# An attention kernel whose loads leave in bursts at TensorE's program fetches, with weights used as loaded and dummy matmuls in the first wait

## The chip, the cores and the metric

One core of one Trainium2 chip. The metric is the device time of one execution in microseconds (us). The engines: TensorE (matmuls; PE in the profile, PEld is its weight load), VectorE (DVE), ScalarE (ACT), GpSimd (POOL), SyncE (SP, which here issues all DMA loads). A kernel's executions scatter by some 3% here, a few by far more (before, in e1's rounds: 439.0 to 454.3 us in 38 runs, 569.6 in one), so each time is given as a median with its range. A run over 1.5% above the fastest of the same kernel is called slow (or in the slow state); verdicts rest on ratios of fast runs made in the same rounds.

## The reference, cut to what matters

Multi-head attention over a cache: x is 8 x 112 x 640, K and V are 8 x 32 heads x 512 x 192, all bf16.

```python
q = transpose((x @ wq).reshape(B, Sq, H, Dh), 0, 2, 1, 3)
scores = einsum("bhqd,bhkd->bhqk", q, k_cache) * (Dh ** -0.5)
p = softmax(scores)
o = einsum("bhqk,bhkd->bhqd", p, v_cache)
return transpose(o, 0, 2, 1, 3).reshape(B, Sq, H * Dh) @ wo
```

## The kernel before

The work is cut into 64 units u, each four heads of one batch entry. A group g of eight units shares a block of wq and wo. Per unit, K is 786 KB and V is 786 KB, each loaded in two halves; there are four buffers for each. On TensorE a unit is: S(u), 96 small matmuls (192 instructions with their weight loads) of query against transposed K; PV(u-1), 16 matmuls of the softmaxed scores against V; some Q or O matmuls (projections for other units); T(u-1), six transposes of the normalised output.

```python
for u in range(NU + 1):                       # TensorE
    if u < NU: do_S(u)
    if u > 0: do_PV(u - 1)
    for it in items_at[u][0]: do(it)          # Q or O
    if u > 0: do_T(u - 1)                     # waits for VectorE's do_NM(u - 1)
    for it in items_at[u][1]: do(it)

for u in range(NU + 1):                       # VectorE
    for t in kts[:2]: do_KT(u + 2, t)         # transposes of K, first wait for its load
    if u > 0: do_NM(u - 1)                    # normalise the output of u - 1
    for t in kts[2:3]: do_KT(u + 2, t)
    # ... O results, last KT
```

In VectorE's program the normalisation of u-1 stands behind the first two K transposes of u+2: if that K is late, so is the normalisation, and with it T(u-1) on TensorE (17.7 us in 17 waits in the trace of before). SyncE issues the loads on events of the work:

```python
for u in range(NU):                           # SyncE
    W(sp, pS, 4 * (u + 1))                    # S(u) is done
    if u + 3 < NU: load_k(u + 3, 0)
    W(sp, pPV, u)                             # PV(u-1) is done
    if u + 3 < NU: load_k(u + 3, 1)
    # ... pieces of wq and wo for later groups
    if items_at[u][0]: after(items_at[u][0][-1])
    if u + 2 < NU: load_v(u + 2, 0)
    if items_at[u][1]: after(items_at[u][1][-1])
    if u + 2 < NU: load_v(u + 2, 1)
```

## Time and profile before

| | before |
|---|---|
| time, median of 3 (range) | 443.99 us (443.99 to 452.72) |
| TensorE busy | 399.6 us, 90% |
| DMA | 118.71 MB, 84.3% of 16 engines' span |
| VectorE's wait for K | 38.3 us in 21 waits |
| TensorE stopped for no visible wait ("issue") | 10.6 us in 9 gaps |
| S block of the first / fourth unit starts | 18.4 / 48.0 us |

Two kinds of line matter. A wait line reads "engine, line, waits for whom: total us, times, longest". "issue" as releaser means that the engine waited for no semaphore. In the trace of before, TensorE's seven such gaps over 0.5 us all stand where a page of its program ends, and it goes on 2.3 to 3.3 us after the start of a program packet (see "How the fetch was read"); so I read them as its own program that had not come, and call them program gaps. The prediction shows these lines. Four more of before are needed later. The waits after the fourth S block alone (48 to 444 us), one group line of the page (busy us, mean ns, idle before) and the page's line of K loads (KB each, median us from issue to landing), each in this order:

```profile
DVE kt L952 <- DMA kr<-in_k_cache_dram: 21.3, 17, 2.1
PE ps L863 <- DVE os L964: 9.1, 15, 1.3
```

```profile
L952 DVE STREAM_TRANSPOSE kt<-kr 128x384 int32<-128x384 int32 x256 | 208.8, 864 | 88.7 <-PE ps L840 50.4 <-DMA kr<-in_k_cache_dram 38.3
```

```profile
kr<-in_k_cache_dram SPq DMA_DIRECT2D x128, 384.0 KB, 4.3
```

### The profile page before, as it was taken

Reading aid. Unit: us, or ns where it says so; the run is one execution under the profiler, and the core shown is the slowest. Engines: PE = TensorE matmul, PEld = TensorE weight load, DVE = VectorE, ACT = ScalarE, POOL = GpSimd, SP = SyncE. Lnnn points to the kernel's source line nnn. Section 1 sums busy time; section 2 is a strip of 40 time slices with the busy share of each in tenths; the row PEclk is TensorE's granted clock in tenths of the full one; section 3 lists DMA queues with packets and bytes.
Section 4 is the critical chain, followed back from the end, with each engine's and each line's share of the span. In section 5 each row is a group of like instructions: output and inputs, shape, how many; then the busy total and the mean of one; then the engine's idle time right before and its main releaser. Section 6 shows DMA issues by size and latency. Waiting matters only on the chain.

```text
span 444.3 us, 20578 instructions
## 1 busy us (share of the span) xinstructions
PE 399.6 (90%) x8920; PEld 293.0 (66%) x8920; DVE 317.5 (71%) x634; ACT 220.8 (50%) x421; POOL 76.8 (17%) x280
## 2 busy tenths in 40 slices
PE   4956999989979999998999899879999999998992
PEld 3534677767767677766676677657677777766771
DVE  2443678768776678886787588756788867887942
ACT  3533355555553655555454555436455565455540
POOL 1040222112211022211221022110222100111110
PEclk9998799999998999999999999989999999999998
DMA  7879799998887989998799899878889988999731
GB/s 263 250 260 332 228 281 299 298 324 278 281 266 245 295 286 299 298 354 262 217 308 297 288 295 284 277 232 257 288 281 306 286 261 272 292 284 298 217 130 36
DMA packets 100655, 120.07 MB, mean 270 GB/s; under 512 B 5584, under 2 KB 84176, under 8 KB 100560
## 3 DMA queue, kind: packets, MB, share of 16 engines
q1 hardware_dynamic: 100560, 118.71, 84.3%
q8 instruction: 71, 1.16, 1.1%
q14 instruction: 24, 0.20, 0.1%
HBM read 117.54 MB, written 1.15 MB: 267 GB/s over the span
## 4 chain that ended last, share of the span: by engine, by line
PE 68%; DMA 16%; DVE 6%; issue 5%; SPq 2%; POOL 1%; ACT 0%; DVEq 0%; POOLq 0%
PE ps L854 17%; PE ps L821 16%; PE ps L840 15%; DMA kr<-in_k_cache_dram 14%; PE ps L805 13%; PE ps L863 5%; DVE os L964 3%; DVE kt L952 3%; PE ps L810 1%; DMA wqr<-in_wq_dram 1%; POOL wqs L1041 1%; DMA xs<-in_x_dram 1%; SPq L1070 1%; SPq L1076 1%; PE ps L785 1%
## 5 line engine op out<-in xcount | busy, mean ns | idle before, releaser
L952 DVE STREAM_TRANSPOSE kt<-kr 128x384 int32<-128x384 int32 x256 | 208.8, 864 | 88.7 <-PE ps L840 50.4
L910 ACT ACTIVATE pT<-ps 128x448 bf16<-128x448 f32 x256 | 118.6, 548 | 79.4 <-PE ps L840 79.4
L821 PE MATMUL ps<-wos,oT 128*128 128x320 bf16 x672 | 109.6, 300 | 1.1 <-ACT oT L919 0.8
L854 PE MATMUL ps<-vs,pT 128*128 128x193 bf16 x1024 | 99.4, 249 | 6.1 <-issue 5.0
L840 PEld LDWEIGHTS ps<-qT,kt 32*128 32x128 bf16 x6144 | 78.5, 94 | 24.3 <-issue 20.2
L805 PE MATMUL ps<-xT,wqs 128*128 128x448 bf16 x420 | 93.5, 359 | 0.9 <-issue 0.8
L840 PE MATMUL ps<-qT,kt 32*128 32x112 bf16 x6144 | 89.1, 210 | 5.3 <-issue 4.6
L854 PEld LDWEIGHTS ps<-vs,pT 128*128 128x128 bf16 x1024 | 83.9, 98 | 12.9 <-issue 7.1
L902 ACT ACTIVATE qT<-ps 128x448 bf16<-128x448 f32 x96 | 52.2, 545 | 66.2 <-PE ps L805 56.9
L821 PEld LDWEIGHTS ps<-wos,oT 128*128 128x128 bf16 x672 | 63.1, 98 | 29.0 <-issue 1.4
L919 ACT ACTIVATE oT<-ps 128x672 bf16<-128x672 bf16 x64 | 46.8, 731 | 63.3 <-PE ps L863 63.2
L1052 POOL TENSOR_SCALAR bad<-rinv 112x4 f32<-112x4 f32 x64 | 14.6, 228 | 322.8 <-DVE rinv L960 322.8
L964 DVE TENSOR_TENSOR os<-ps,rinv 112x768 bf16<-112x768 f32 x64 | 61.3, 958 | 2.5 <-DVE rinv L960 0.4
L805 PEld LDWEIGHTS ps<-xT,wqs 128*128 128x128 bf16 x420 | 39.9, 99 | 29.0 <-issue 3.3
L863 PE MATMUL ps<-ident,os 112*128 112x112 bf16 x384 | 30.4, 216 | 17.9 <-DVE os L964 17.7
L863 PEld LDWEIGHTS ps<-ident,os 112*128 112x128 bf16 x384 | 21.0, 99 | 34.9 <-DVE os L964 34.0
L978 DVE TENSOR_TENSOR acc<-ps,acc 128x320 f32<-128x320 f32 x84 | 40.3, 480 | 1.5 <-PE ps L821 1.5
L1041 POOL COPY wqs<-wqr 128x384 bf16<-128x384 bf16 x70 | 33.2, 507 | 24.3 <-DMA wqr<-in_wq_dram 22.4
L957 DVE TENSOR_REDUCE sm<-ps 112x4 f32<-112x8 f32 x64 | 10.1, 158 | 11.7 <-PE ps L854 11.5
L810 PE MATMUL ps<-xT,wqs 128*32 128x448 bf16 x240 | 15.8, 422 | 1.2 <-ACT xT L891 0.8
L1053 POOL TENSOR_SCALAR bad<-rinv 112x4 f32<-112x4 f32 x64 | 14.5, 226 | 4.0
L960 DVE RECIPROCAL rinv<-sm 112x4 f32<-112x4 f32 x64 | 11.4, 178 | 3.4
(30 smaller groups left out, 52.0 us busy)
## 6 DMA issues: line engine op xcount, KB each, us to landing
kr<-in_k_cache_dram SPq DMA_DIRECT2D x128, 384.0 KB, 4.3
vs<-in_v_cache_dram SPq DMA_DIRECT2D x128, 384.0 KB, 4.6
wos<-in_wo_dram SPq DMA_DIRECT2D x48, 160.0 KB, 4.3
wqr<-in_wq_dram SPq DMA_DIRECT2D x35, 192.0 KB, 4.4
out_dram<-xs SPq DMA_DIRECT2D x7, 160.0 KB, 1.9
wqs<-in_wq_dram SPq DMA_DIRECT2D x1, 960.0 KB, 6.5
xs<-in_x_dram SPq DMA_DIRECT2D x1, 640.0 KB, 4.3
xs<-in_x_dram SPq DMA_DIRECT2D x1, 480.0 KB, 7.9
```

The costliest lines, as they stand in the source:

```text
L805: mm = pe.matmul(ps[:, bank(it), 0:HQ], wqs[:, g % 2, dc, 128 * c:128 * (c + 1)], rhs, start=(dc == 0), stop=(dc == DC - 1))
L821: mm = pe.matmul(ps[:, bank(it), 0:HO], oT[:, c, 128 * m:128 * (m + 1)], wos[:, g % 2, c, HO * h:HO * (h + 1)], start=(c == 0), stop=(c == 5))
L840: mm = pe.matmul(ps[:, a, SQ * t:SQ * (t + 1)], kt[u % 2][p, t, c // 2, :, c % 2], qT[g % 2][p, c, SQ * b:SQ * (b + 1)], start=(c == 0), s ...
L854: mm = pe.matmul(pv[:, k, e, o0:o0 + DH + 1], pT[u % 2][:, a, t, :], vs[u % NV][:, a, t // 2, v0:v0 + DH + 1], start=(t == 0), stop=(t == ...
L863: mm = pe.transpose(psb[:, 4, o0:o0 + SQ], os_[u % 2][:, 128 * j:128 * (j + 1)], ident[0:SQ, 0:SQ])
L902: act.activation(qT[g % 2][:, c, HQ * h:HQ * (h + 1)], ps[:, bank(it), 0:HQ], ACTF.Copy).then_inc(aQ, 1)
L910: act.activation(pT[u % 2][:, a, :, 0:SQ], ps[:, a, 0:4 * SQ].rearrange("p (t q) -> p t q", t=4), ACTF.Exp, scale=scale).then_inc(aEX, 1)
L919: act.activation(oT[:, :, SQ * b:SQ * (b + 1)].rearrange("p (k c) q -> p k c q", k=2), src.rearrange("p k (c q) -> p k c q", c=3), ACTF.Co ...
L952: dve.transpose(dst, src).then_inc(vKT, 1)
L964: dve.tensor_tensor(os_[u % 2][:].rearrange("p (k e d) -> p k e d", k=2, e=2), pv[0:SQ, :, :, 1:1 + DH], rinv[:, u % 4, :].rearrange("p (k ...
L978: ins = dve.tensor_tensor(ob[:, m, cs] if g == NG - 1 else acc[:, m, cs], src, acc[:, m, cs], op=ALU.add)
L1041: ins = gp.tensor_copy(wqs[:, g % 2, dc, :].rearrange("p (k e a i) -> p e k a i", k=3, e=2, a=4)[:, e], wqr[:, dc, :].rearrange("p (a k i ...
```

## The change

The intent: let a count of TensorE's own instructions tell when it has entered a new page of its program (256 instructions by the places of the gaps, see "How the fetch was read"; a program packet is 16.3 KB), and let SyncE issue everything that is due just then. The next page's fetch should then be ahead of the burst in the queues, and the burst over before the fetch after it. Besides: wq is read by strided matmul operands as it was loaded, where GpSimd had reordered it; K is transposed in the matching order; nine dummy matmuls fill the first wait, meant to have TensorE's clock up when work comes (the first three Q took 1.86 us each before, and 1.0 us with the dummies).

```diff
+    FIRST = 194
+            def put(emit, first, us):            # every matmul and transpose goes through this
+                at[0] += len(held) // 2
+                held.clear()
+                mm = emit()
+                if first and at[0] >= 256 * len(fetch) + FIRST:
+                    mm.then_inc(pF, 1)           # "a page was entered"
+                    fetch.append(at[1])
+                at[0] += 2
   ... cut ...
-                    for a in range(4):           # first weight block: quarter-width matmuls
-                        w0 = DH * a + 64 * (c // 2) + c % 2
-                        mm = pe.matmul(ps[32 * a:32 * a + 32, bank(it), 0:HQ], wqs[:, 0, dc, w0:w0 + 63:2], rhs, ...)
+                    mm = matmul(0.188, ps[:, bank(it), 0:HQ], wqs[:, g % 2, dc, c::6], xT[:, dc, HQ * h:HQ * (h + 1)], ...)
   ... cut ...
+            for _ in range(9):
+                matmul(0.43, ps[:, 7, :], zero[:, 0:128], zero[:], start=True, stop=True)
   ... cut ...
-                src = kr[u % NK][:, t:16:4, :].bitcast(I32).rearrange("p s (c i) -> p c s i", c=3)
+                src = kr[u % NK][:, t:16:4, :].bitcast(I32).rearrange("p s (i c) -> p c s i", c=3)
   ... cut: GpSimd's reorder() goes; x tiles in other PSUM banks ...
-            for u in range(NU):
-                W(sp, pS, 4 * (u + 1))
-                if u + 3 < NU:
-                    load_k(u + 3, 0)
   ... cut: the whole loop over events ...
+            loads = [(0.0, load_k, 2, 0), (0.0, load_k, 2, 1), (0.3, load_v, 1, 0), (0.3, load_v, 1, 1)]
+            loads += [(0.1, load_wq, 1, c) for c in range(DC)] + [(1.0, load_wo, 0, c) for c in range(6)]
+            for u in range(NU):
+                g, b = divmod(u, B)
+                if u + 3 < NU:
+                    loads += [(u, load_k, u + 3, 0), (u + 0.25, load_k, u + 3, 1)]
+                if u + 2 < NU:
+                    loads += [(u + 0.5, load_v, u + 2, 0), (u + 0.75, load_v, u + 2, 1)]
   ... cut: wq and wo likewise ...
+            loads.sort(key=lambda w: w[0])
+            for n, us in enumerate(fetch):
+                ...                              # place = unit reached by then
+                due = [w for w in loads if w[0] <= place + 0.45]
+                if due:
+                    sp.wait_ge(pF, n + 1)
+                for _, fn, p0, p1 in due:
+                    fn(p0, p1)
+                loads = loads[len(due):]
```

## The prediction

> **What bounds the kernel now.** I read the page first (engine shares, slices, queues), then the table of waits, then the timeline of TensorE around its gaps, then the DMA view and the busy table for short stretches there. The page:

> ```profile
> PE 399.6 (90%) x8920; PEld 293.0 (66%) x8920; DVE 317.5 (71%) x634; ACT 220.8 (50%) x421; POOL 76.8 (17%) x280
> GB/s 263 250 260 332 228 281 299 298 324 278 281 266 245 295 286 299 298 354 262 217 308 297 288 295 284 277 232 257 288 281 306 286 261 272 292 284 298 217 130 36
> q1 hardware_dynamic: 100560, 118.71, 84.3%
> q8 instruction: 71, 1.16, 1.1%
> ```

> TensorE is the bound, with DMA close behind: 118.71 MB in 444 us, and one slice that reached 354 GB/s. At that rate the bytes would need 335 us, so DMA need not bind if it is kept fed. The q8 line is the program itself: 1.16 MB / 71 is 16.3 KB a packet, and 17,840 matmuls and weight loads / 71 is 251 per packet.

> The table of waits says what stops TensorE:

> ```profile
> DVE kt L952 <- DMA kr<-in_k_cache_dram: 38.3, 21, 7.5
> PE ps L863 <- DVE os L964: 17.7, 17, 4.6
> PE ps L785 <- DMA xs<-in_x_dram: 5.2, 1, 5.2
> PE ps L854 <- issue: 5.0, 4, 2.1
> PE ps L840 <- issue: 4.6, 3, 2.8
> PE ps L805 <- issue: 0.8, 1, 0.8
> PE ps L821 <- issue: 0.2, 1, 0.2
> ```

> VectorE stands 38.3 us because K tiles land late; 17.7 us of that reaches TensorE, since the normalisation (L964) stands behind the K transposes in VectorE's order. The four "issue" rows (10.6 us) are gaps in which TensorE waits for no semaphore. The longest, in the timeline of TensorE:

> ```profile
> 290.96 1.35 PE L840 MATMUL ps<-qT,kt 32*128 32x112 bf16 x94
> 295.15 0.22 PE L840 MATMUL ps<-qT,kt 32*128 32x112 bf16 x2 [2.84 <-issue]
> 295.38 1.58 PE L854 MATMUL ps<-vs,pT 128*128 128x193 bf16 x16
> 296.76 2.07 PE L805 MATMUL ps<-xT,wqs 128*128 128x448 bf16 x5
> ```

> It stops two matmuls short of a block's end, where no wait stands in the program. The DMA view of 292.7 to 293.9 us has this line, which the view of 290.9 to 292.7 has not:

> ```profile
> q8 instruction: 1, 0.02, 4.9%
> ```

> So a program packet moved inside the gap, behind 1.8 us of data at full queues: TensorE had run out of program. After such gaps it also runs at half clock (the Q above took 2.07 us; elsewhere 1.11). The busy table of chosen stretches gives the granted clock:

> ```profile
> 33.90:37.30 3.40, 3.40 (x70) 1.86 (x71) 1.26 (x2) 1.27 (x2) 0.00 (x0) 0.51 0.94 270
> 44.10:50.90 6.80, 5.46 (x111) 3.87 (x112) 2.96 (x8) 1.74 (x4) 0.65 (x3) 0.50 0.76 246
> 296.70:300.10 3.40, 3.40 (x14) 1.70 (x12) 2.44 (x6) 0.54 (x1) 0.65 (x3) 0.50 0.79 242
> ```

> With a fourth stretch like the last (at 132.8), half of the busy time in these is lost: (3.4 + 5.5 + 3.4 + 3.2) / 2 = 7.7 us.

> [...]

> **The change, part by part.**

> *Loads tied to the program fetch.* TensorE's first accumulating matmul after each 256-instruction boundary bumps a semaphore; SyncE then issues all loads due. The fetch request is ahead of the burst, and the burst should be over before the next fetch. A page is about one unit of work (a unit is 272 to 280 instructions), so 5.3 us or a little more. Working through the list that the kernel builds, usual bursts are 3 to 6 loads, 1.2 to 1.95 MB, or 3.4 to 5.5 us at 354 GB/s, plus 1.5 us or so to land (the 160 KB stores, on quiet queues, take 1.9 us in all). The fullest spill 1 to 1.5 us into the next page, whose fetch (about 1 us) still has 4 us of room. So I expect the 10.6 us of "issue" to fall to about 2. K halves go out 0.8 to 1.4 units before VectorE may use them, near the front of the burst when they are late, so against 4.3 us from issue to landing they are mostly in time: of 9.3 us waits L863 <- L964 after the third unit I keep 4.

> *The start.* Nine 512-column matmuls at half clock (about 0.43 us each, 3.9 us) fill the 5.2 us in which TensorE waits for x. They cost nothing; the clock should be full near 6.6 to 8 us in place of 13.4. The first Q can't start before the first weights are there (issued at 1.24, 6.5 us to landing: 7.8). Today it starts at 8.34, the first three Q run at 1.86 us each, and the first S starts at 18.41. Full-width Q cost 5 x 0.189 = 0.945 against 20 quarter-width ones in 1.04. New order: three Q from 7.9 to 10.7, the late x tiles land near 11, Q, Q, transpose, Q to 14; K transposes of the first unit follow the fifth x tile and end near 13.7. First S at about 14.4: 4 us won.

> *The first three units.* Today S starts at 18.4, 23.2, 36.3 and 48.0: the third and fourth wait 4.65 and 3.98 us for late K and run half-clocked. At full rate the units cost S 1.29 + three Q 2.84 = 4.1; + PV 1.46 = 5.6; + transposes and the rest = 6.0. So S would start at 14.4, 18.6, 24.2, 30.2. The first burst is heavy, though (12 loads, 3.7 MB, 10.6 us at 354): V of the second unit is near its end and lands about 1 us after its need, and the next fetch waits behind it. I add 3 us: 33.2 against 48.0, 14.8 us won, with the start's 4 in it.

> *Weights as loaded.* The 70 copies on GpSimd (33.2 us, off the path except near 24.9 to 29.5) vanish; so does the wait of loads for them. The strided weight load hides behind a 0.187 us matmul; K transposes should keep 0.86 us. I count 0 for both.

> *After the fourth S (48.0).* 396.3 us remain today. In them: "issue" 9.8 (10.6 less 0.9 at 24.7, rounded), waits for L964 9.3 (17.7 less 4.65 and 3.98, with short ones that I counted from the timeline), half clock (2.9 + 3.2 + 3.4) / 2 = 4.8. Together 23.9, leaving 372.4 if all went. I keep 2 of issue, 4 of K waits, 0 of clock: 378.4.

> Sum: 33.2 + 378.4 = 411.6; I say **411 us** (before / after 1.08). If nothing at all were kept it would be 30.2 + 372.4 = 402.6.

> **The rivals.**

> *VectorE becomes the bound.* It is busy 317.5 / 64 = 5.0 us a unit, against 5.7 to 6.0 of TensorE. If the stride of 12 bytes made the 256 transposes a quarter slower (0.86 to 1.08), it would need 5.8 us a unit, and any late K would go straight through: 420 to 430 us. For it: VectorE's narrow room. Against: [...]the destination is already written at a stride of 4 int32.

> *DMA becomes the bound.* Loads end about 25 us before the kernel does, so at 411 us they must average 118.7 / 380 = 312 GB/s, where the page shows 245 to 332 in most slices. Gaps between bursts waste rate, and bursts that overlap catch up with the fetch again. Then K is late once more, and the time is 418 to 430. For it: 84.3% share already. Against: the 354 slice, and slices below 260 fall where loads were held back by events.

> *The alignment misses.* The count assumes 62 instructions before the kernel's own first one. If a boundary lies elsewhere, the burst goes ahead of the fetch at every page instead of some, and "issue" grows: 71 pages x 0.5 us would be 35 us, at or above 435. Against: the constant looks fitted[...].

> **Range and chances.** The floor of 402.6 and the small rivals set 403 to 424. All named gains together are 41 us and 2% is 8.9, so most of them would have to fail: faster 0.93, same 0.05, slower 0.02.

> **What would show it.** Right: "issue" before TensorE under 3 us; VectorE's wait for K from 38.3 to under 15; no half clock after the start; first S near 14.4 and fourth near 33; K transposes still 0.86 us; Q at 0.95 us. Wrong: transposes near 1.1 us or Q above 1.1 (stride); issue gaps at every page (alignment); DMA share near 100% with K waits as today (DMA bound).

## The result, and the profile after

The changed kernel took 460.81 us (median of 4, 456.92 to 465.36) against 444.93 us of the kernel before in the same rounds: **3.3% slower**. All ratios in this document are the mean time of one kernel's fast runs over that of the other's fast runs of the same rounds, so they are not quite the ratio of the medians: here 1.0335, 95% interval 1.0230 to 1.0441. The first profile fell in the slow state, so I ran the unedited kernel once more, later in the study:

> The changed kernel once more, without any edit, because its one profile fell in the slow state and its few times scatter, so that the padded run could not be set against it. Both theories: time 456 to 463. If page phase is worth time, this is 4 us or more above the padded run (457.8, scattered 453 to 463) in a profile of the fast state, that is at or above 456 against 451.6; if it is not, the two profiles agree within 2 us. K wait 50 to 60 and issue 17 to 22 in a fast profile.

It took 454.16 us (453.64 to 461.30), ratio 1.0325 (1.0205 to 1.0445): the same verdict, a little under the times that I had expected. Its profile is of the fast state, and the lines below are of it. First the page: busy time, bandwidth in 40 slices, queues, and the shares of the chain that ended last.

```profile
PE 401.5 (89%) x8749; PEld 303.2 (67%) x8749; DVE 320.0 (71%) x635; ACT 220.3 (49%) x421; POOL 43.5 (10%) x210
GB/s 280 246 345 249 309 285 298 246 255 305 305 302 288 266 243 234 298 266 316 290 306 267 221 268 337 288 303 259 325 193 264 268 303 284 283 263 277 188 62 35
q1 hardware_dynamic: 100560, 118.71, 81.4%
PE 44%; DMA 28%; DVE 12%; issue 8%; SPq 6%; ACT 1%; DVEq 0%
```

TensorE is no busier (401.5 against 399.6 us) and DMA moves the same bytes at a lower share (81.4 against 84.3%). Time went into waiting. The waits, to be set against those in the prediction:

```profile
DVE kt L974 <- DMA kr<-in_k_cache_dram: 53.8, 34, 5.3
PE ps L803 <- DVE os L986: 20.3, 25, 5.4
PE ps L800 <- issue: 14.9, 9, 3.0
PE ps L800 <- ACT pT L932: 2.4, 1, 2.4
PE ps L803 <- DMA xs<-in_x_dram: 0.2, 1, 0.2
```

VectorE's wait for K rose from 38.3 to 53.8 us instead of falling below 15; TensorE's gaps for lack of program rose from 10.6 to 14.9 us instead of falling to 2 (to 17.3 with the row for ScalarE's pT, see below). The wait for x is gone, as meant (5.2 to 0.2). After the fourth S block alone (42.6 to 452 us) the two K rows are, against 21.3 and 9.1 above:

```profile
DVE kt L974 <- DMA kr<-in_k_cache_dram: 38.9, 30, 2.6
PE ps L803 <- DVE os L986: 12.7, 23, 1.2
```

Half of all units now find their K late. The page's line of K loads says part of why: a K half takes 5.1 us to land where it took 4.3.

```profile
kr<-in_k_cache_dram SPq DMA_DIRECT2D x128, 384.0 KB, 5.1
```

The start, in the timeline of TensorE (start, duration, what, count, idle before), then one line of VectorE's:

```profile
8.10 3.01 PE L800 MATMUL ps<-xT,wqs 128*128 128x448 bf16 x15 [0.88 <-ACT xT L913]
...
15.82 1.36 PE L800 MATMUL ps<-qT,kt 32*128 32x112 bf16 x96 [0.73 <-ACT qT L924]
...
23.27 2.06 PE L800 MATMUL ps<-xT,wqs 128*128 128x448 bf16 x10
30.76 0.74 PE L803 MATMUL ps<-ident,os 112*128 112x112 bf16 x6 [5.44 <-DVE os L986]
...
42.58 2.03 PE L800 MATMUL ps<-qT,kt 32*128 32x112 bf16 x96
```

```profile
27.95 1.53 DVE L974 STREAM_TRANSPOSE kt<-kr 128x384 int32<-128x384 int32 x2 [2.69 <-DMA kr<-in_k_cache_dram]
```

The first three Q take 1.0 us each in place of 1.86, and the first S block starts at 15.8 us (18.4 before). But the fourth unit's K lands at 27.9 us; the normalisation stands behind its transposes, T waits 5.44 us, and the clock falls (0.54 granted from 30.7 to 34.1 us). The fifth unit's K, asked for after V and six pieces of wo, lands at 37.5 us and T waits again (2.08 us). The fourth S block starts at 42.6 us, and runs at half clock itself (2.03 us for what takes 1.36). Last, the program: one gap later on, and the granted clock and bandwidth of five stretches (columns: window, length, busy of PE, PEld, DVE, ACT, POOL, granted clock, DMA share, GB/s).

```profile
159.01 1.36 PE L800 MATMUL ps<-qT,kt 32*128 32x112 bf16 x96
163.42 2.71 PE L800 MATMUL ps<-vs,pT 128*128 128x193 bf16 x16 [3.04 <-issue]
```

```profile
30.70:34.10 3.40, 3.34 (x59) 1.95 (x63) 1.49 (x3) 1.28 (x2) 0.00 (x1) 0.54 1.08 369
41.00:44.40 3.40, 3.40 (x98) 2.23 (x99) 0.72 (x2) 1.09 (x2) 0.00 (x0) 0.55 0.14 42
163.80:167.20 3.40, 3.40 (x20) 2.55 (x19) 0.96 (x4) 0.00 (x0) 0.44 (x2) 0.54 0.52 160
334.50:337.90 3.40, 3.16 (x19) 2.74 (x20) 0.34 (x2) 0.00 (x0) 0.00 (x0) 0.54 0.36 96
423.20:426.60 3.40, 3.40 (x18) 1.97 (x17) 2.50 (x8) 0.00 (x0) 0.65 (x3) 0.54 0.12 15
```

The gaps are as long as before (3.04 us here, 2.84 the longest then), and the clock still falls after some (0.54 after the one shown). In the last column DMA moves 369 GB/s in the first half-clock stretch, then 42, 160 and 96 (the last comes when nearly everything is loaded). In three such stretches of the kernel before it moved 242 to 270 GB/s, but in the fourth, after a program gap, only 129:

```profile
133.10:136.50 3.40, 3.40 (x19) 2.69 (x20) 0.74 (x4) 0.00 (x0) 0.29 (x2) 0.54 0.38 129
```

By the program, loads that leave only when TensorE enters a page stop when TensorE stops. What that costs is not shown by these few stretches.

One more program gap goes under another name. At 332.34 us TensorE stops for 2.41 us, again where a page ends, and goes on 2.51 us after a packet. The profile puts it down to ScalarE's pT (the row in the waits above), but the PV that follows needs only pT of the unit before, for which S had already waited. So it is a program gap too. The same row stands in most other runs, with one exception of 0.7 us (in e10) at page ends and 2.2 to 3.0 us after a packet; the kernel before has none.

### The profile page after: what moved, and what is told of

Its sections match the earlier page's. It is cut to its first block, busy times and chain, and to the rows that moved or that the text cites. A ratio compares the mean times of both kernels' runs of the same rounds, so it can differ in the third digit from the quotient of the medians.

```text
span 463.7 us, 19950 instructions
## 1 busy us (share of the span) xinstructions
PE 402.9 (87%) x8749; PEld 303.9 (66%) x8749; DVE 320.4 (69%) x635; ACT 220.1 (47%) x421; POOL 43.1 (9%) x210
## 3 DMA queue, kind: packets, MB, share of 16 engines
q1 hardware_dynamic: 100560, 118.71, 80.0%
## 4 chain that ended last, share of the span: by engine, by line
PE 48%; DMA 26%; DVE 12%; issue 9%; SPq 3%; ACT 1%; DVEq 0%
PE ps L800 43%; DMA kr<-in_k_cache_dram 26%; DVE kt L974 7%; PE ps L803 4%; DVE os L986 4%; SPq L1085 1%; SPq L1099 1%; SPq L1091 1%; ACT pT L932 1%; DVE rinv L982 1%; SPq L1078 0%; ACT oT L941 0%; DVE ps L983 0%; ACT xT L913 0%; DVE sm L979 0%
## 5 line engine op out<-in xcount | busy, mean ns | idle before, releaser
L800 PE MATMUL ps<-wos,oT 128*128 128x320 bf16 x672 | 111.3, 304 | 3.5 <-issue 2.6
L800 PE MATMUL ps<-xT,wqs 128*128 128x448 bf16 x480 | 107.2, 361 | 1.8 <-ACT xT L913 0.8
L800 PEld LDWEIGHTS ps<-vs,pT 128*128 128x128 bf16 x1024 | 83.7, 98 | 27.2 <-issue 18.6
L800 PEld LDWEIGHTS ps<-qT,kt 32*128 32x128 bf16 x6144 | 77.7, 93 | 18.9 <-issue 14.8
L800 PE MATMUL ps<-qT,kt 32*128 32x112 bf16 x6144 | 87.8, 209 | 0.7 <-ACT qT L924 0.7
L800 PEld LDWEIGHTS ps<-xT,wqs 128*128 128x128 bf16 x480 | 56.8, 126 | 26.0 <-issue 3.3
L1062 POOL TENSOR_SCALAR bad<-rinv 112x4 f32<-112x4 f32 x64 | 14.4, 225 | 399.3 <-DVE rinv L982 399.3
L803 PEld LDWEIGHTS ps<-ident,os 112*128 112x128 bf16 x384 | 21.3, 100 | 44.0 <-DVE os L986 42.6
L1000 DVE TENSOR_TENSOR acc<-ps,acc 128x320 f32<-128x320 f32 x84 | 39.9, 475 | 2.4 <-PE ps L800 2.2
L979 DVE TENSOR_REDUCE sm<-ps 112x4 f32<-112x8 f32 x64 | 10.1, 158 | 23.4 <-PE ps L800 23.4
L1065 POOL TENSOR_TENSOR cnt<-cnt,bad 112x8 f32<-112x8 f32 x64 | 12.8, 200 | 5.3
L1000 DVE TENSOR_TENSOR xs<-ps,acc 128x320 bf16<-128x320 f32 x14 | 6.3, 482 | 2.2 <-PE ps L800 2.2
```

The lines of the kernel that those rows point to most:

```text
L800: return put(lambda: pe.matmul(out, w, m, start=start, stop=stop, **kw), start and not stop, us)
L803: return put(lambda: pe.transpose(out, m, eye), first, 0.05)
L1000: ins = dve.tensor_tensor(ob[:, m, cs] if g == NG - 1 else acc[:, m, cs], src, acc[:, m, cs], op=ALU.add)
L1062: gp.tensor_scalar(bad[:, 0, :], rinv[:, u % 4, :], LO, None, op0=ALU.is_lt)
L1065: gp.tensor_tensor(cnt[:], cnt[:], bad[:], op=ALU.add).then_inc(gC, 1)
```

## The experiments

Fourteen runs, one of them the changed kernel again, in five calls (no e5 is on record). A first table gives the results together; "gaps" is the sum of TensorE's issue rows, and after the plus the program gaps that the profile puts down to pT. Times of different calls are compared through their ratios to the kernel before.

| run | what | median (range), us | ratio, 95% interval | K wait | gaps |
|---|---|---|---|---|---|
| before | | 444.1 to 446.1 by call | 1 | 38.3 | 10.6 |
| changed | repeat | 454.2 (453.6 to 461.3) | 1.0325 (1.0205 to 1.0445) | 53.8 | 14.9 + 2.4 |
| e1 | changed, loads on old events | 443.6 (438.4 to 451.4) | 0.9993 (0.9953 to 1.0034) | 34.0 (slow) | 18.3 + 2.2 (slow) |
| e2 | changed, bursts 64 instructions later | 457.6 (455.2 to 460.9) | 1.0293 (1.0193 to 1.0393) | 44.0 | 22.3 + 3.0 |
| e3 | changed, K earlier in the bursts | 440.7 (437.8 to 504.0) | 0.9943 (0.9894 to 0.9993) | 13.3 | 17.2 + 2.7 |
| e4 | changed, slivers of K and V (wrong result) | 423.9 (423.3 to 424.5) | 0.9552 (0.9442 to 0.9662) | 12.8 | 5.4 + 2.9 |
| e6 | e1 with K a unit earlier | 434.8 (429.9 to 438.8) | 0.9792 (0.9615 to 0.9968) | 9.3 | 12.8 + 4.9 |
| e7 | e3, bursts later and fitted in size | 437.5 (433.5 to 444.5) | 0.9877 (0.9841 to 0.9913) | 16.8 (slow) | 20.9 + 2.4 (slow) |
| e8 | changed, pages shifted | 457.8 (453.4 to 463.0) | 1.0363 (1.0184 to 1.0542) | 52.9 | 10.4 + 0.9 |
| e9 | e6, pages shifted | 427.6 (426.5 to 433.7) | 0.9723 (0.9611 to 0.9836) | 10.1 | 9.6 + 1.9 |
| e10 | e3, pages shifted | 434.2 (427.4 to 439.8) | none: two fast runs | 9.0 | 12.1 + 1.6 |
| e11 | before with K a unit earlier | 436.3 (429.8 to 446.5) | 0.9845 (0.9799 to 0.9891) | 8.6 (slow) | 13.9 + 2.3 (slow) |
| e13 | e9, new order of first loads, wo late | 435.1 (431.3 to 439.2) | 0.9855 (0.9747 to 0.9963) | 4.8 | 18.8 + 1.9, of them 7.0 for wo |
| e14 | e13 without the shift | 440.2 (437.8 to 443.1) | 0.9974 (0.9943 to 1.0005) | 4.4 | 25.0 + 4.1, of them 7.4 for wo |
| e15 | e13, wo back | 424.6 (421.2 to 431.3) | 0.9550 (0.9492 to 0.9607) | 5.5 | 12.2 + 1.3 |

"(slow)" marks a profile that fell in the slow state; those waits are not compared closely. All results but e4's are correct.

### Which part of the change costs: e1 and e2

e1 undoes the scheduling and keeps the rest (start, strided weights, dummies).

```diff
-            for n, us in enumerate(fetch): ...   # bursts
+            for u in range(NU):
+                W(sp, pS, 4 * (u + 1))
+                if u + 3 < NU:
+                    load_k(u + 3, 0)
+                ...                              # the loop of the kernel before, pieces of wq later in a group
```

> The changed kernel with the loads issued on the old events (after S, after PV, after each half of Q and O), everything else as changed. If the bursts are what costs, this is faster than the kernel before by the start's gain: 4 us from the start, 2 to 8 from the first units, so 432 to 441 us, issue waits near 10 us and VectorE's wait for K near 38 us as before. If the strided weights, the K stride or the dummy matmuls cost, it stays at 450 or above.

e2 keeps the bursts and moves them within the page: `FIRST = 194` becomes `FIRST = 258`, 64 instructions later.

> The count moved 64 instructions later (258 in place of 194), so that the burst can't be ahead of a fetch request that leaves up to 64 instructions past the boundary. Theory A (the request leaves late[...], and the burst gets ahead of it): fetch packets move within 1 us of the burst's start on all pages, issue waits fall from 19 us to under 8, while K is as late or later (VectorE's wait for K 58 to 75 us): 445 to 460 us. Rival B (the burst is too large for its page, whoever is first): issue waits stay at 15 us or rise, 460 us or more.

e1 is the kernel before to within 0.5%; so the bursts are the whole loss, 3.3%, and the other parts together neither cost nor win. That misses my 432 to 441 us. The start did win: e1's fourth S block is at 39.2 us, 8.8 us earlier than in the kernel before. By the end this is lost again; e1's gaps are 20.5 us against 10.6, though in a slow profile. e2 is no better than the change: gaps 22.3 us. The median fetch lag went from 1.57 to 2.56 us. So if bursts stood ahead of their own page's fetch, 64 instructions did not cure it; sent later, as I read it, they only reach further into the next page.

### Late K, and the floor: e3 and e4

e3 lets K leave three quarters of a unit earlier; a free K buffer is there, since there are four.

```diff
-                    loads += [(u, load_k, u + 3, 0), (u + 0.25, load_k, u + 3, 1)]
+                    loads += [(u - 0.75, load_k, u + 3, 0), (u - 0.5, load_k, u + 3, 1)]
   ... and K of the third unit ahead of the weights, V of the second a little earlier ...
```

> K made due 0.75 units earlier, so that it stands ahead of V in each burst or one burst earlier; count at 194 as in the change. If late K is the larger part: VectorE's wait for K falls from 58 us to under 20, the transposes' wait for the normalisation from 26 us to under 10, and the time to 438 to 446 us with the issue waits left near 19 us. If the bursts only reorder a saturated queue, V becomes late in its place (TensorE's PV waits for V) and the time stays above 452.

e4 loads only slivers of K and V from the fifth unit on. Its result is wrong on purpose; it shows the schedule with little DMA (30.4% share).

```diff
+                n = 8 * DH if u < NK else 32      # K: 32 of 1536 elements per row and half
+                n = 2 * DH if u < NV else 16      # V likewise
   ... cut: n in the loads themselves ...
```

> Wrong result on purpose: from the fifth unit on, K and V loads bring only a sliver (64 and 32 bytes a partition), so the queues are nearly empty. Shows the floor and the fetch alone. Theory A: a fetch still costs request to first instruction about 2.5 us, so pages that begin with slow work and end in S keep issue waits of 0.5 to 1.5 us each, 3 to 8 us in all; the kernel runs 402 to 412 us. Rival B: no issue waits at all. If the strided weights cost TensorE anything, the time is above 415 with TensorE busy.

The waits in e3 and in e4:

```profile
PE ps L800 <- issue: 17.2, 10, 3.9
DVE kt L974 <- DMA kr<-in_k_cache_dram: 13.3, 4, 4.6
PE ps L803 <- DVE os L986: 4.9, 3, 2.6
```

```profile
DVE kt L974 <- DMA kr<-in_k_cache_dram: 12.8, 4, 3.7
PE ps L803 <- DVE os L986: 6.0, 3, 4.9
PE ps L800 <- issue: 5.4, 8, 1.3
```

e3 wins 3.7% against the change (0.9943 / 1.0325 = 0.963) by one reordering, with program gaps no smaller (17.2 for 14.9 us). So K in time is alone enough to make up the loss. Measured from the traces after the first five units: for the second half of each K, how long before VectorE could first use it (the end of the S block before last) it was issued, how long it took, and what was left. Each is a median over 59 units.

| | issued before need | issue to landing | left | late by over 0.1 us |
|---|---|---|---|---|
| before | 4.27 us | 4.30 us | +0.13 us | 18 units |
| changed | 5.22 us | 5.32 us | -0.21 us | 32 units |
| e3 | 9.77 us | 5.57 us | +3.81 us | 1 unit |
| e6 | 10.96 us | 4.45 us | +6.22 us | none |

The change did issue K earlier, by 0.95 us; but in the bursts it lands 1.02 us slower; as I read it, because V and weights of the same moment share the queue. It had stood at the edge before, and went over it.

e4 shows that even with little data in the queues 8.3 us of gaps stay (5.4 + 2.9); the rest, 17.3 - 8.3 = 9.0 us in the changed kernel, comes with the data. e4's time missed: 423.9 us for 402 to 412, over the 415 that I had set as a sign of costly strided weights. The weights are not the reason, since a Q matmul took 355 ns in e4 and 359 in the kernel before. The first units, which load in full, reach the fourth S block only at 39.9 us, and of the 381.7 us that follow 8.3 are gaps.

### Events or bursts once K is early: e6, e7, e11

e6 is e1 with K of unit u+4 asked for where K of u+3 was:

```diff
+            for h in range(2):
+                load_k(3, h)                      # ahead of the loop
             for u in range(NU):
                 W(sp, pS, 4 * (u + 1))
-                if u + 3 < NU:
-                    load_k(u + 3, 0)
+                if u + 4 < NU:
+                    load_k(u + 4, 0)
   ... the second half likewise ...
```

> The changed kernel's start and weights, loads on the old events, but each K one unit of work earlier (K of unit u+4 is asked for when the S block of unit u is done; V and the weights as before). Theory A (two separate losses: K asked for too late, and program fetches that stand behind loads): VectorE's wait for K falls from 34.0 to under 15 us, TensorE's wait for the normalisation from 13.1 to under 6, the issue gaps stay at 15 to 20 us because the bytes in front of the fetches are the same; time 432 to 438 against 443.6 of the run with the old events. Rival B (K is late because the transfer queues are full, whenever it is asked for): the K wait stays near 30 us and the time stays 441 to 446.

e7 takes e3's bursts, sends them 48 instructions later and fits their size to the time until the next page's request, as I then pictured it.

```diff
+    FIRST = 242
+                ask = when(256 * (n + 1) + 242)
+                need = when(256 * (n + 2) + 194) - 2.4
+                room = 0.33 * (max(min(ask + 3.0, need), ask) - us - 0.5)    # MB
   ... take loads in order while there is room ...
```

> The bursts of the run with early K, with two more rules: the burst leaves 48 instructions later (after the point at which I think the request for the next program page leaves), and its size is what fits into the time until the next request leaves, so that short pages get small bursts (1.2 to 1.5 MB) and long ones large bursts. Theory A (the request leaves late, some 45 instructions into a page, and then waits behind what is left of the last burst): issue gaps fall from 17.2 to 5 to 9 us, K wait stays near 13, time 425 to 433. Rival B (the size of bursts is not what delays the fetch; sending them 48 instructions later only makes their tail meet the next fetch, as in the run that moved the burst 64 instructions): issue stays at 15 to 22 us, time 438 to 445.

e11 makes e6's edit in the kernel before, and nothing else.

> The kernel before with one edit: each K is asked for a unit earlier, nothing else of the change. Theory A (late K is a loss of its own, and the start with dummies and full-width weights adds to it): VectorE's wait for K from 38.3 to under 15, TensorE's wait for the normalisation from 17.7 to under 8, the issue gaps stay near 10; time 434 to 440, some 2 to 6 us above the same edit in the changed kernel with old events. Rival B (K can't be earlier here because the loads of the second weight block wait for GpSimd's copies and hold the queue): the K wait stays above 25 and the time 441 to 446.

e6 behaved as theory A said; its gaps are in the range of 15 to 20 us only with the two under pT (17.7 in all). Waits of e6:

```profile
PE ps L800 <- issue: 11.8, 12, 2.4
DVE kt L974 <- DMA kr<-in_k_cache_dram: 9.3, 3, 5.1
PE ps L803 <- DVE os L986: 5.6, 2, 4.8
```

e7's gaps (20.9 us, in a slow profile) and fetch lag (median 2.54 us) speak against the picture behind it: fitting the bursts behind a later trigger did not clear the way of the fetches. e11 takes 1.6% off the kernel before with one edit of six lines, and its fast runs (mean 433.3 us) equal those of e6 (433.1 us), with ratios whose intervals overlap (the runs are of different calls). No gain of the changed start and weights can be shown here; theory A's 2 to 6 us between the two is not seen.

### Where pages end: e8, e9, e10

The gaps cluster: a few units in a row have one each, then many have none. A unit is about 273 instructions in the changed kernel (17,498 / 64), so page ends move through the unit by some 17 a unit. The pages that end in a gap all begin in slow work and hold a whole S block, 192 instructions that are gone in 1.3 us. In the changed kernel these ten pages lasted 1.9 to 4.0 us without their gaps; the median of all pages is 5.6 us. If the place of page ends matters, shifting all pages by a constant should change the gaps. e8 does it with more, but shorter, dummies: 83 more matmuls, 166 instructions.

```diff
-            for _ in range(9):
+            for _ in range(4):
                 matmul(0.43, ps[:, 7, :], zero[:, 0:128], zero[:], start=True, stop=True)
+            for _ in range(88):
+                matmul(0.04, ps[:, 7, 0:32], zero[:, 0:128], zero[:, 0:32], start=True, stop=True)
```

> The changed kernel with 4 wide dummy matmuls and 88 narrow ones in place of 9 wide ones: 166 more instructions ahead of the first real one, which shifts where the program's pages end in the work; nothing else is changed. Theory A (the gaps come where a page ends in slow work shortly before an S block, so their number depends on the phase of pages to units; counted from the trace, a fetch that takes 3.4 us would cost 13.8 us at the present phase and about 10 at this one): issue gaps 10 to 15 us against 19.1, K wait 45 to 60 as now, time 446 to 455 against 457 to 462. Rival B (phase doesn't matter, the gaps come from the load of the queues alone): issue 18 to 21 us, time 456 to 463.

e9 and e10 put the same edit into e6 and e3.

> The run with the old events and each K a unit earlier, with the 88 narrow dummy matmuls that shift the pages. Theory A (phase and early K act independently): issue gaps 5 to 9 us against 11.8, K wait near 9, time 427 to 432 against 434.8. Rival B (what the shift saves in gaps comes back as other waits, as it seemed to in the padded changed kernel): issue falls, but the time stays 433 to 437.

> The bursts with K earlier (440.7 us) and the 88 narrow dummies. Theory A: issue gaps from 17.2 to 8 to 11 us, K wait 10 to 20, time 429 to 435. Rival B: issue falls, the time stays 438 to 442.

The gaps and the K rows in e8:

```profile
DVE kt L976 <- DMA kr<-in_k_cache_dram: 52.9, 33, 5.2
PE ps L803 <- DVE os L988: 23.2, 23, 6.1
PE ps L800 <- issue: 10.4, 6, 3.0
```

The gaps fell as expected, 14.9 to 10.4 us, but the time did not (profiles 451.6 and 452.1 us): TensorE's wait for the normalisation grew by 2.9 us, and its half clock before the end of the work from 17.1 to 23.9 us. That while K is late much of what a gap costs would have been waited for anyway is my reading, not shown. With K early the shift seemed to pay, 434.8 to 427.6 us from e6 to e9, but those are runs of different calls, and the ratios to the kernel before (0.979 and 0.972) overlap; e13 and e14 settle it. e10 stays above e9 (434.2 against 427.6 in the same call, though e10 has two fast runs, 427.4 and 432.4): bursts are not shown to be better than events when both have K early.

### The start: e13, e14, e15

The fourth S block was at 39.8 us in e9, because K of the third and fourth unit stand behind the second weight block, which is first used near 36 us. e13 reorders the first loads; e14 is the same without the shift of pages, in the same rounds.

```diff
-            for c in range(DC):
-                load_wq(1, c)
-            after(order[5])
             for h in range(2):
                 load_k(2, h)
+            for h in range(2):
+                load_k(3, h)
+            after(order[5])
             for h in range(2):
                 load_v(1, h)
-            for h in range(2):
-                load_k(3, h)
+            for c in range(DC):
+                load_wq(1, c)
   ...
-                if u == 0:                        # first block of wo
+                if u in (2, 3):                   # three pieces each
```

> The fastest run so far (old events, each K a unit earlier, pages shifted: 427.6 us, fourth S block at 39.8 us, where VectorE waited for the K of the third and fourth unit) with the first loads in another order: K of the third and fourth unit straight after V of the first, then V of the second unit, then the second weight block (first used near 36 us) and the first output weights two units later. Theory A (the start misses my prediction because of the order of the first loads, not because the queue is full): third S block at 26 to 29 us against 33.8, fourth at 32.5 to 36 against 39.8, VectorE's K wait 4 to 7 us; time 420 to 424. Rival B (the queue is full from 3 to 30 us, so something else is late instead, V or weights): fourth S block stays at 38 or later, time 426 to 429.

> The same new order of the first loads, without the 88 narrow dummies (the 9 wide ones in their place). On the same chip and in the same rounds as the padded one, so that the pair tells what the shift of the pages is worth once K comes in time. Theory A (phase is worth some 5 us): issue gaps 3 to 5 us above the padded run, time 426 to 430. Rival B (the earlier difference of the pair, 434.8 against 427.6, was one of chips or rounds): the two agree within 2 us.

Both reached the fourth S block at 34.5 us, and then lost it: in e13 the first O matmul stood 7.0 us at 39.4 us, for wo that I had moved too late. The profile calls it issue, since one landing is missing in the trace, but it is not at a page's end. The pair still answers its question: every fast run of e13 (431.3 to 437.1) is below every run of e14 (437.8 to 443.1), and gaps without the wait for wo are 13.7 against 21.7 us. The shift of pages is worth about 6 us once K comes in time. e15 puts wo back into the first two units.

```diff
-                if u in (2, 3):
-                    for c in range(3 * u - 6, 3 * u - 3):
+                if u in (0, 1):
+                    for c in range(3 * u, 3 * u + 3):
```

> The padded run with the new order of the first loads, with the first output weights asked for in the first two units instead of the third and fourth. In the run before this one they came too late: TensorE's first use of them stood 7.0 us at 39.4 us (put down to issue, since the landing of one weight load is missing from the trace) and then ran at half clock. Theory A (that was my error in the edit, and the rest of the order is good): no gap at 39 us, third S block at 27 to 29 us and fourth at 34 to 36, fifth at 40.5 to 43; time 420 to 425. Rival B (the queue is too full in the first 45 us for all of it, whatever the order): a wait of 3 us or more for K or weights stays before the fifth S block, time 427 to 432.

424.6 us, **4.5% faster than the kernel before**, correct, the best version found. The chain that ended last, the waits and the start (third, fourth and fifth S block, a gap in each):

```profile
PE 90%; issue 3%; DMA 2%; DVE 1%; ACT 1%; SPq 1%; DVEq 0%
```

```profile
PE ps L800 <- issue: 11.8, 15, 2.6
DVE kt L976 <- DMA kr<-in_k_cache_dram: 5.5, 2, 3.0
PE ps L803 <- DVE os L988: 0.8, 1, 0.8
```

```profile
27.63 1.11 PE L800 MATMUL ps<-qT,kt 32*128 32x112 bf16 x74
29.23 0.47 PE L800 MATMUL ps<-qT,kt 32*128 32x112 bf16 x22 [0.49 <-issue]
...
34.22 1.01 PE L800 MATMUL ps<-qT,kt 32*128 32x112 bf16 x67
36.14 0.55 PE L800 MATMUL ps<-qT,kt 32*128 32x112 bf16 x29 [0.90 <-issue]
...
41.05 0.91 PE L800 MATMUL ps<-qT,kt 32*128 32x112 bf16 x58
42.82 0.67 PE L800 MATMUL ps<-qT,kt 32*128 32x112 bf16 x38 [0.86 <-issue]
```

TensorE sets 90% of the chain, where the changed kernel had 44% and a DMA share of 28%. Program gaps remain, 13.5 us of them.

## Why the prediction was wrong

It said 411 us, 8% faster; the kernel was 3.3% slower. Its sum against the fast profile, with the gaps (14.9 + 2.4) and the K waits after the fourth S block from the rows above, the half clock as half the busy time of its three late stretches, (3.40 + 3.16 + 3.40) / 2, and the rest as what is left of the span:

| term | predicted | measured | off by |
|---|---|---|---|
| fourth S block starts | 33.2 | 42.6 | 9.4 |
| issue gaps kept | 2 | 17.3 | 15.3 |
| K waits kept (T behind the normalisation) | 4 | 12.7 | 8.7 |
| half clock kept | 0 | 5.0 | 5.0 |
| the rest after the fourth S block | 372.4 | 374.5 | 2.1 |
| sum | 411.6 | 452.1 | 40.5 |

**Issue gaps: the step failed.** It read: "The fetch request is ahead of the burst, and the burst should be over before the next fetch", with 4 us of room for the fullest bursts. The typical fetch did improve (median lag 2.07 to 1.57 us). The worst ones did not (longest 5.6 before, 6.0 changed). Two things were missed. First, pages are not all "5.3 us or a little more": the ten that end in a gap ran out after 1.9 to 4.0 us, so the 4 us of room were not there, and e8 and the pair e13 and e14 show that the place of page ends alone moves 6.0 to 8.0 us of gaps. Second, 8.3 us of gaps stay with little data in the queues (e4), so 2 was out of reach.

**K: mechanism right, one number wrong.** The prediction gave K halves 0.8 to 1.4 units of lead, and they had 5.22 us, inside that. It set this "against 4.3 us from issue to landing", the number of the kernel before. In a burst it was 5.32 us in the median (the median of both halves is 5.1 in the page). The burst that moves K forward also slows it. e3 and e6 show what a larger lead is worth.

**The start: first half right, second wrong.** The clock came up early, as I had estimated (the first three Q took 1.0 us each for 1.86; the clock record of the changed kernel's first, slow profile has full clock from 6.8 us, that of before from 13.4); the first S block came at 15.8 us for 14.4. The heavy first burst was seen ("12 loads, 3.7 MB") and given 3 us; the fourth S block came 12.4 us after its unhindered time (42.6 - 30.2; 1.4 of it was there at the first S block). Not all of that is the burst's: e1, on the old events, gets there at 39.2 us, for it too asks for the second weight block before this K. V of the second unit was named as the one to be late; it was K of the fourth, its second half issued behind five pieces of wq and landing at 27.9 us, and K of the fifth at 37.5. The estimate of 33.2 us was not too bold for the hardware: e15, with another order, reached 34.2.

**No half clock after the start: wrong,** three stretches after the fourth S block, after some of the long gaps. The length of a gap alone does not tell which: in the changed kernel the granted clock was 0.54 after 2.30 us without work (at 420.8 us), and 1.00 after 2.56 us (at 76.4 us). All its half-clock stretches start whole multiples of 3.41 us apart (30.40, 40.64, 163.52, 334.19, 422.93 and 446.83 us). In the 3.41 us before each of them TensorE stood idle for 1.85 us or more; the gap at 76.4 us lies across two such stretches of 3.41 us, with 1.79 us in the first.

**Weights as loaded cost nothing: right.** This was my estimate; no trace of before showed either stride. K transposes, now at a stride of 3 int32, took 871 ns for 864, the full-width Q 359 ns a matmul as in the kernel before. The weight loads, now at a stride of 6 bf16, did get longer (126 for 99 ns), but lie under the matmuls: Q did not get slower. Lines of the changed kernel:

```profile
L974 DVE STREAM_TRANSPOSE kt<-kr 128x384 int32<-128x384 int32 x256 | 210.8, 871 | 88.5 <-DMA kr<-in_k_cache_dram 53.8 <-PE ps L800 34.6
L800 PE MATMUL ps<-xT,wqs 128*128 128x448 bf16 x480 | 106.5, 359 | 1.8 <-ACT xT L913 0.9 <-issue 0.6 <-ACT qT L924 0.3
L800 PEld LDWEIGHTS ps<-xT,wqs 128*128 128x128 bf16 x480 | 56.5, 126 | 25.9 <-issue 3.0 <-DVE xT L1006 1.0 <-ACT qT L924 0.7
```

**The rivals.** VectorE bound by the stride: no. Alignment missed at every page: no, ten gaps in 70 pages. "DMA becomes the bound" had the right symptom, late K from overlapping bursts, and the wrong sign: the DMA share fell, to 81.4%. It was order and latency, not rate: e15 ran at 87.0%.

**The chance of 0.93** rested on 41 us of separate gains, "most of them would have to fail". They were not separate: gaps, K waits and most of the start were all expected from the same loads schedule, and fell with it (e1).

**Still open.** When exactly a page's request leaves TensorE, and why a fetch comes later with more data in the queues (median lag 0.84 us in e4, 2.07 in the kernel before), is not shown; two kernels (e2, e7) built on a guess about this failed. Why e1, on the old events, has more gaps than the kernel before is not shown either; its stream is shorter (8749 matmuls for 8920), so its pages end elsewhere.

## What to carry to other kernels

A load's lead must be compared with its latency under the schedule that you plan, not the one that you measured: grouping loads lengthened it here, from 4.30 to 5.32 us for the second half of a K. Before building a clever schedule, list for every load its first use and issue in that order; here one unit more of lead for K, which a free buffer allowed all along, was worth more than the whole change (e11 takes 1.6% off, the change adds 3.3%). Program gaps depended here on where pages end in the work: shifting them by 166 instructions alone took 6.0 us (e8) and 8.0 us (e13 against e14) of gaps away.
